# A two-product MLP beside a windowed attention: blocks of 512 tokens in place of 256, and the second product token tile by token tile

## The chip, the cores and the metric

The kernel runs on one core of one Trainium2 chip. That core has TensorE (matrix products, with its own queue of weight loads, called PEld in the profile), VectorE (DVE), ScalarE (ACT), GpSimd (POOL), and SyncE (SP), which here only issues DMAs. Each engine works through its own instructions in the order in which the program gives them; engines wait for each other through semaphores. The metric is the device time of one execution in microseconds (us). Lower is better.

## The reference, cut to what matters

There are 2048 tokens of width 576. They are normalized, and two branches are added to the input:

```python
x = A_x                                       # 1 x 2048 x 576
xn = _layernorm(x, axis=-1)
# branch A: 32 heads of 18; each token looks at itself and at 7 tokens, 2 apart, before it
qkv = xn @ wqkv;  logits = q . k over the window * 18**-0.5;  o = softmax(logits) . v;  A = o @ wo
# branch B
h = jnp.maximum(xn @ w1, 0)                   # 576 -> 4608
B = h @ w2                                    # 4608 -> 576
return x + A + B
```

All is float32. The kernel gets precision near float32 from TensorE's fast float32 mode by splitting every operand into a high part and a low part, which is what the rounding of the high part left over. A product is then three products: high x high, low x high and high x low.

## The kernel before

**Tiling.** Tokens are taken in two phases of 1024 (even and odd tokens, so that the dilated window becomes a plain one). A phase has 8 token tiles of 128 tokens. For branch B a phase has 4 blocks of 256 tokens (two token tiles each). The 4608 columns of w1 are 36 F tiles of 128, and three F tiles make a chunk, so there are 12 chunks. The innermost loops are: phase, chunk, block, F tile of the chunk. One turn of these four loops is a *slot*; there are 288.

**One slot.** `h_mm` (line 438) makes the first product for one F tile and one block: 14 matmuls (list `TERMS`: 576 rows are four and a half tiles of 128, high and low) with a 128x128 tile of w1 as weights, streaming the block's 256 columns of x^T (tile xT) into a PSUM tile `ph`. Then ACT writes the high part of the relu (`hhi`, line 447) and DVE the low part (`hlo`, line 448). `o_mm` (line 453) makes the second product for the same F tile: for both token tiles of the block, six matmuls of 288 columns with 128x128 pieces of hhi or hlo as weights and w2 streaming, into a PSUM tile `po` per token tile. The two `po` collect over the three F tiles of the chunk; at the third, DVE adds them to the token tile of x in SBUF (line 471), which thus becomes the output. `h_mm` runs two slots ahead of `o_mm` (`LAG`).

**The order.** All engines' instructions are issued in an order written out by hand. A slot issues: the weight splits that are due (`run_splits`), `h_mm`, the steps that `at` has put on this slot, `o_mm`, the steps that `late` has put there, and background work (`run_bg`). A plan gives each step its slot:
- *weights*: `w1_task`, `w2_task`, `wq_tasks`, `wo_tasks` queue a load from HBM into a staging tile `st` (SP) and, at their slot, a split (`two`, line 146: ACT copies the high part; line 143: DVE subtracts for the low part). `stage_more` keeps `AHEAD` = 3 loads ahead in four staging tiles; they are used in order of their step numbers.
- *x*: `load_x` (SP), `stats` (mean and variance on DVE, then two small POOL steps), `norm` (on DVE, line 259, or with `act` on ACT, lines 256 and 257; a last small ACT copy, line 261, follows), `make_xt` (five TensorE transposes, then ACT high parts, lines 276 and 278, and DVE low parts, lines 277 and 279).
- *branch A*: four units of 8 heads, 27 slots apart: `qkv_tile` (14 matmuls of 432 columns for each token tile into a `pm`, three ACT copies), then `attention`, whose DVE steps wait in a list `bg`. `run_bg` issues them as long as the program's own estimate of DVE's time is at most a margin ahead of its estimate of TensorE's. `wo_a` and `wo_b` make the last product of branch A.

PSUM has 8 banks: two `po` tiles of two banks, two `ph`, and two `pm` for everything else.

**The start.** Before the first slot the tiles of x and the first weights are loaded, tiles 0 and 1 are normalized and transposed, and the first w1 tiles are split. The list `HEAD` then places the statistics, norms and transposes of tiles 2 to 7 on slots -2 to 5, and `HEADW` the first six weight splits on slots -5 to 1. The first block needs only tiles 0 and 1, the second only 2 and 3. 24 transposes of the identity (`WARM`) run on TensorE at the very start.

Of the kernel before, what the change touches and what calls it, by code (L numbers as in the profile page):

```python
# [20 lines left out]
NTB = 4  # L21
TBN = 256
# [4 lines left out]
LAG = 2  # L27
# [3 lines left out]
HEADW = (-5, -2, -1, 0, 0, 1)  # L31

HEAD = (
    (-2, 0, 'stats', 3),
    (-2, 1, 'xt', 2, True),
    (-1, 0, 'stats', 4),
    (-1, 1, 'norm', 3, True),
    (0, 0, 'xt', 3, False),
    (0, 0, 'norm', 4, True),
    (0, 0, 'stats', 6),  # L40
    (0, 1, 'stats', 5),
    (1, 1, 'norm', 5, False),
    (1, 1, 'xt', 4, False),
    (2, 1, 'xt', 5, False),
    (2, 1, 'norm', 6, True),
    (2, 1, 'stats', 7),
    (4, 0, 'norm', 7, True),
    (4, 1, 'xt', 6, False),
    (5, 1, 'xt', 7, False),
)  # L50
HALO = ((0, 112), (112, 127))
# [4 lines left out]
def tile_body(ctx: ExitStack, tc: tile.TileContext, x, wqkv, wo, w1, w2, out):  # L56
# [11 lines left out]
    SPC = NTB * C  # L68
# [13 lines left out]
    stp = pool("stp", 4)  # L82
    hp = pool("hp", LAG + 2)
    prp = pool("prp", 2)
    lgp = pool("lgp", 2)
# [3 lines left out]
    ps_h = pool("ps_h", 2, space=PSUM)  # L89
    ps_m = pool("ps_m", 2, space=PSUM)  # L90
# [20 lines left out]
    def mm(o, l, r, start, stop, n):  # L111
        nc.tensor.matmul(o, l, r, start=start, stop=stop)  # L112
        t["pe"] += n / 2400.0 + 0.002
# [7 lines left out]
    AHEAD = 3  # L121
# [142 lines left out]
    def transpose_split(src, last, hi, mix, lo, free=False):  # L264

        if free:
            pa, pb = (ps_o.tile([P, 2, 512], F32, name="po")[:, 0, :] for _ in range(2))
            pa, pb = pa.rearrange("p (k c) -> p k c", k=KT), pb[:, 0:P]
        else:
            pa = ps_m.tile([P, KT, P], F32, name="pm")  # L270
            pb = ps_m.tile([P, P], F32, name="pm")
# [11 lines left out]
    def make_xt(ph, i, free=False):  # L283
        tb, h = divmod(i, 2)
# [12 lines left out]
    def qkv_tile(ph, u, i):  # L297
# [9 lines left out]
        tb, h = divmod(i, 2)  # L307
        xt = XT[ph, tb]
        pq = ps_m.tile([P, 3, UD], F32, name="pm")
# [97 lines left out]
    def wo_a(ph, i):  # L407
        assert (ph, i) in ready, (ph, i, len(bg))
        o = QO[ph][:, i, :]
        od = tmp.tile([P, 2, DR], F32, name="od")  # L410
# [5 lines left out]
    def wo_b(ph, i):  # L416
        d, w = OT.pop((ph, i)), WO[ph]
        po = [ps_m.tile([P, D2], F32, name="pm") for _ in range(2)]
# [15 lines left out]

    slots = [(ph, c, tb, f) for ph in range(NPH) for c in range(NCH) for tb in range(NTB) for f in range(C)]
    H, PO = {}, {}

    def h_mm(n):
        ph, c, tb, f = slots[n]
        w, xt = W1[ph, c, f], XT[ph, tb]  # L440
        pt = ps_h.tile([P, TBN], F32, name="ph")
# [7 lines left out]
        t["dve"] = max(t["dve"], t["pe"] + 0.6)  # L449
        dve(TBN)  # L450
        H[n] = (hi, lo)
# [76 lines left out]
    for i in range(AHEAD + 2, NI):  # L528
        load_x(0, i)
# [56 lines left out]
```

## Time and profile before

| what | value |
|---|---|
| time, median of 3 runs | 1194.94 us (1194.33 to 1195.93) |
| the profiled execution's own time | 1194.74 us |
| its span in the trace | 1193.0 us |
| TensorE busy | 1183.8 us (99%) |
| weight loads (PEld) busy | 1172.8 us (98%) |
| DVE busy | 812.5 us (68%) |
| ACT busy | 310.5 us (26%) |
| POOL busy | 40.1 us (3%) |
| DMA moved | 75.67 MB, mean 63 GB/s |

How to read the profile: each row of the groups is one kind of instruction, as line, engine, operation, output<-inputs with the partitions x elements, a count, then total busy time, mean ns of one, and idle time of the engine just before them with what ended it. In the timeline a row is a start, a length, and a group of like instructions; the length runs to the modelled end of the last one, and matmuls overlap, so the pace of matmuls is read from one start to the next. The chain of waits follows the work back from the last instruction, at each step to what released it.

### The profile page before, as it was taken

How to read it: one execution, taken by the hardware profiler on the slowest of the kernel's cores; microseconds unless marked ns; L12 is line 12 of the kernel's file. 1: busy time of each engine (PE TensorE's matmuls, PEld its weight loads, DVE VectorE, ACT ScalarE, POOL GpSimd, SP SyncE). 2: the span in 40 equal slices, each digit the busy share in tenths (PEclk: the TensorE clock that was granted, in tenths of full speed). 3: DMA queues.
4: the chain of work that ended last, by engine and by line, in shares of the span. 5: the costliest groups of instructions: out<-in, count | busy, mean ns of one | idle time of the engine just before them, and what ended most of it. 6: DMA issues, size and time to landing. Idle time of an engine off the chain costs nothing.

```text
span 1193.0 us, 21739 instructions
## 1 busy us (share of the span) xinstructions
PE 1183.8 (99%) x9016; PEld 1172.8 (98%) x9016; DVE 812.5 (68%) x1269; ACT 310.5 (26%) x790; POOL 40.1 (3%) x63
## 2 busy tenths in 40 slices
PE   8999999999999999999999999999999999999998
PEld 7999999999999999999999999999999999999998
DVE  7516875888687578875573278858767875886732
ACT  5422222131222222322233123122221322222210
POOL 2000000010000000000120000000100000000000
PEclk9999999999999999999999999999999999999999
DMA  5312122130321311402242113031302312212002
GB/s 172 84 32 82 42 76 55 38 107 1 98 58 44 86 33 43 114 11 73 91 130 74 46 54 90 22 85 29 86 21 79 83 38 79 63 42 73 21 1 80
DMA packets 84883, 75.67 MB, mean 63 GB/s; under 512 B 6592, under 2 KB 68288, under 8 KB 84784
## 3 DMA queue, kind: packets, MB, share of 16 engines
q1 hardware_dynamic: 82256, 66.08, 19.7%
q10 hardware_dynamic: 2528, 8.20, 2.4%
q8 instruction: 71, 1.16, 0.4%
q14 instruction: 28, 0.23, 0.1%
HBM read 61.34 MB, written 4.72 MB: 55 GB/s over the span
## 4 chain that ended last, share of the span: by engine, by line
PE 98%; DVE 1%; SPq 0%; ACT 0%; DMA 0%; issue 0%; DVEq 0%; ACTq 0%
PE ph L112 39%; PE po L112 38%; PE pm L112 20%; PE pm L273 1%; PE pm L274 0%; DMA st<-in_w 0%; SPq L235 0%; DVE pr L380 0%; DVE pr L373 0%; SPq L157 0%; SPq L162 0%; SPq L161 0%; PE po L273 0%; ACT xn L257 0%; ACT xn L256 0%
## 5 line engine op out<-in xcount | busy, mean ns | idle before, releaser
L112 PE MATMUL ph<-xT,w1t 128*128 128x256 f32 x4032 | 514.2, 279 | 1.3 <-ACT xT L276 0.6
L112 PEld LDWEIGHTS ph<-xT,w1t 128*128 128x128 f32 x4032 | 491.6, 188 | 2.0 <-ACT xT L276 0.8
L112 PE MATMUL po<-w2t,hhi 128*128 128x288 f32 x2304 | 400.5, 296 | 0.4 <-DVE w2t L143 0.3
L112 PEld LDWEIGHTS po<-w2t,hhi 128*128 128x128 f32 x2304 | 337.0, 188 | 2.0 <-DVE w2t L143 0.5
L447 ACT ACTIVATE hhi<-ph 128x256 fp32r<-128x256 f32 x288 | 110.2, 382 | 531.8 <-PE ph L112 512.5
L112 PE MATMUL po<-w2t,hlo 128*128 128x288 f32 x1152 | 244.7, 293 | 0.0
L448 DVE SCALAR_TENSOR_TENSOR hlo<-ph,hhi 128x256 fp32r<-128x256 f32 x288 | 121.7, 423 | 169.1 <-ACT hhi L447 167.8
L471 DVE TENSOR_TENSOR x<-po,x 128x576 f32<-128x576 f32 x192 | 143.9, 757 | 69.8 <-PE po L112 66.3
L112 PE MATMUL pm<-wq,xT 128*128 128x432 f32 x896 | 185.5, 358 | 0.0
L112 PEld LDWEIGHTS po<-w2t,hlo 128*128 128x128 f32 x1152 | 183.7, 188 | 0.0
L112 PEld LDWEIGHTS pm<-wq,xT 128*128 128x128 f32 x896 | 163.8, 188 | 5.6
L343 DVE TENSOR_TENSOR pr<-qo,k 128x1152 f32<-128x1152 f32 x64 | 85.9, 1349 | 0.0
L373 DVE TENSOR_TENSOR pr<-lg,v 128x1152 f32<-128x1152 f32 x64 | 85.0, 1352 | 0.3
L346 DVE TENSOR_REDUCE lg<-pr 128x64 f32<-128x1152 f32 x64 | 85.0, 1343 | 0.0
L143 DVE TENSOR_TENSOR w2t<-st,w2t 128x576 fp32r<-128x576 f32 x72 | 54.3, 755 | 45.0 <-ACT w2t L146 44.7
L380 DVE TENSOR_TENSOR pr<-pr 128x288 f32<-128x288 f32 (+1 forms) x128 | 70.5, 602 | 0.1
L143 DVE TENSOR_TENSOR w1t<-st,w1t 128x640 fp32r<-128x640 f32 x72 | 59.0, 820 | 15.0 <-ACT w1t L146 14.8
L146 ACT ACTIVATE w2t<-st 128x576 fp32r<-128x576 f32 x72 | 49.1, 684 | 45.0 <-PE po L112 31.0
L146 ACT ACTIVATE w1t<-st 128x640 fp32r<-128x640 f32 x72 | 53.0, 737 | 13.2 <-DMA st<-in_w 13.2
L312 ACT ACTIVATE k<-pm 128x144 f32<-128x144 f32 x64 | 18.7, 292 | 142.8 <-PE pm L112 142.6
L112 PE MATMUL pm<-wq,oT 128*128 128x288 f32 x352 | 51.7, 299 | 0.0
L112 PEld LDWEIGHTS pm<-wq,oT 128*128 128x128 f32 x352 | 47.9, 188 | 1.7
(63 smaller groups left out, 398.0 us busy)
## 6 DMA issues: line engine op xcount, KB each, us to landing
st<-in_w SPq DMA_DIRECT2D x72, 288.0 KB, 3.0
st<-in_w SPq DMA_DIRECT2D x72, 256.0 KB, 3.0
st<-in_wqkv SPq DMA_DIRECT2D x32, 216.0 KB, 3.0
st<-in_w SPq DMA_DIRECT2D x144, 32.0 KB, 2.7
out<-x SPq DMA_DIRECT2D x16, 288.0 KB, 2.1
x<-in_x SPq DMA_DIRECT2D x15, 288.0 KB, 3.9
k<-k ACTq DMA_DIRECT2D x8, 441.0 KB, 3.9
v<-v ACTq DMA_DIRECT2D x8, 441.0 KB, 4.6
```

Source lines behind the costliest of these rows:

```text
L112: nc.tensor.matmul(o, l, r, start=start, stop=stop)
L143: nc.vector.tensor_tensor(lo, src, f32(hi), op=ALU.subtract)
L146: nc.scalar.activation(hi, src, AF.Copy)
L273: nc.tensor.transpose(pa[:, k, :], src[:, k * P : (k + 1) * P], ident)
L312: nc.scalar.activation(k[:, W - 1 + i, :], pq[:, 1, :], AF.Copy)
L343: nc.vector.tensor_tensor(pr[i], q, window(k, i), op=ALU.mult)
L346: nc.vector.tensor_reduce(lg[:, i], pr.pop(i).rearrange(heads, d=Dh), axis=AX.X, op=ALU.add)
L373: nc.vector.tensor_tensor(pr[i].rearrange(heads, d=Dh), e, window(v, i).rearrange(heads, d=Dh), op=ALU.mult)
L380: nc.vector.tensor_tensor(o, z[:, 0:n], z[:, n : 2 * n], op=ALU.add)
L447: nc.scalar.activation(hi, pt, AF.Relu)
L448: nc.vector.scalar_tensor_tensor(lo, pt, 0.0, f32(hi), op0=ALU.max, op1=ALU.subtract)
L471: nc.vector.tensor_tensor(acc, PO[k][:, :, 0:D2], acc, op=ALU.add)
```

## The change

The names changed are few, but the order of nearly all work changes with them.
- A block is 512 tokens: four token tiles (`TBT`), two blocks in a phase (`NTB`). `h_mm` streams 512 columns into one whole PSUM bank, and the relu's two parts are 128x512 each.
- A block's turn (`SPB`) is six slots. In the first three, `h_mm` runs for the F tiles 1 and 2 of this block and F tile 0 of the next. In the last three the second product runs, a third of it in each (`o_mm`, now drawing from the generator `o_pieces`): token tile by token tile, and for each token tile all three F tiles, so that one `po` is filled by 18 matmuls in a row and then added to x. A phase still has 144 slots, and the slots of the weights' and of branch A's steps are nearly those of before.
- PSUM: `ph` and `pm` share one pool of four banks (`ps_x`). Staging tiles are 3 in place of 4, loads ahead 2 in place of 3, and the softmax tile `lg` has one buffer.
- `run_bg` is called inside `h_mm` after every four matmuls and inside `o_mm` after every six, with one margin of 2.0 us; the estimates of TensorE's and DVE's time have new constants.
- The start is written out anew. F tile 0 and F tile 1 of the first block are made in halves of 256 columns (`A`, `B`), with the transposes of tiles 2 and 3 between them; the second product of the first block stands in slots 3 to 5, and the transposes of tiles 5, 6 and 7 stand at the head of its three slots. The third w2 tile's split has the step number 3.
- The x tiles of the second phase are prepared on slots that fit the new blocks.

The diff, cut to its core:

```diff
-NTB = 4
-TBN = 256
+NTB = 2
+TBT = 4
+TBN = TBT * P
-LAG = 2
-HEADW = (-5, -2, -1, 0, 0, 1)
+HEADW = (-9, -8, -7, -6, -5, 3)
 HEAD = (
...
+    (3, 0, "xt", 5),
+    (3, 0, "stats", 6),
+    (3, 1, "norm", 6),
+    (3, 1, "stats", 7),
+    (4, 0, "xt", 6),
+    (4, 1, "norm", 7),
+    (5, 0, "xt", 7),
 )
+MARGIN = 2.0
-    SPC = NTB * C
+    SPB = 2 * C
+    SPC = NTB * SPB
-    stp = pool("stp", 4)
-    hp = pool("hp", LAG + 2)
+    stp = pool("stp", 3)
+    hp = pool("hp", C + 1)
-    lgp = pool("lgp", 2)
+    lgp = pool("lgp", 1)
-    ps_h = pool("ps_h", 2, space=PSUM)
-    ps_m = pool("ps_m", 2, space=PSUM)
+    ps_x = pool("ps_x", 4, space=PSUM)
-        t["pe"] += n / 2400.0 + 0.002
+        t["pe"] += n / 2250.0 + 0.0025
-    AHEAD = 3
+    AHEAD = 2
...
+    def h_mm(n, f, cols=slice(0, TBN)):
+        ph, c, tb = blocks[n]
         w, xt = W1[ph, c, f], XT[ph, tb]
+        if cols.start == 0:
+            PH[n, f] = ps_x.tile([P, TBN], F32, name="px")
+        pt = PH[n, f]
         for j, (a, b) in enumerate(TERMS):
             wb = w[:, b // 5, (b % 5) * P : (b % 5 + 1) * P]
-            mm(pt, wb, xt[:, a, :], j == 0, j == len(TERMS) - 1, TBN)
+            mm(pt[:, cols], wb, xt[:, a, cols], j == 0, j == len(TERMS) - 1, cols.stop - cols.start)
+            if j % 4 == 3:
+                run_bg(MARGIN)
+        if cols.stop < TBN:
+            return
...
+    def o_pieces(n):
+        ph, c, tb = blocks[n]
+        for k in range(TBT):
+            po = ps_o.tile([P, 2, 512], F32, name="po")
             cs = slice(k * P, (k + 1) * P)
+            for f in range(C):
+                hi, lo = H[n, f]
+                w = W2[ph, c, f]
+                for j, (l, b) in enumerate(((hi, 0), (hi, 1), (lo, 0))):
+                    for h in range(2):
+                        mm(
+                            po[:, h, 0:D2], l[:, cs], w[:, b, h * D2 : (h + 1) * D2],
+                            f == 0 and j == 0, f == C - 1 and j == 2, D2,
+                        )
+                        if f == C - 1 and j == 2 and h == 1:
+                            i = TBT * tb + k
+                            acc = X[ph, i].rearrange("p (h c) -> p h c", h=2)
+                            nc.vector.tensor_tensor(acc, po[:, :, 0:D2], acc, op=ALU.add)
...
+                        yield
...
+    def o_mm(n, s):
+        if s == 0:
+            PO[n] = o_pieces(n)
+        for i in range(6 * TBT):
+            next(PO[n])
+            if i % 6 == 5:
+                run_bg(MARGIN)
...
+                plan.append((HEADW[f] if first else s - 8 + (0, 4, 5)[f], w1_task, ((ph, c, f), c * C + f)))
+                plan.append((HEADW[C + f] if first else s + (-2, 0, 1)[f], w2_task, ((ph, c, f), c * C + f)))
...
+    run_splits(-9)
     norm(0, 0)
     norm(0, 1)
     stats(0, 2)
...
     norm(0, 2, True)
+    h_mm(0, 0, A)
+    stats(0, 3)
+    run_splits(-8)
+    make_xt(0, 2, True)
+    norm(0, 3, True)
+    h_mm(0, 1, A)
+    run_splits(-7)
+    make_xt(0, 3, True)
+    h_mm(0, 0, B)
+    stats(0, 4)
+    h_mm(0, 1, B)
+    norm(0, 4, True)
+    h_mm(0, 2)
+    run_splits(-6)
+    stats(0, 5)
+    make_xt(0, 4)
+    run_splits(-5)
+    norm(0, 5)
...
+    for n in range(C, len(blocks) * SPB):
         run_splits(n)
+        q, s = divmod(n, SPB)
+        if s < C - 1:
+            if n == SPB:
+                h_mm(1, 0)
+            h_mm(q, s + 1)
+        elif s == C - 1 and q + 1 < len(blocks):
+            h_mm(q + 1, 0)
         for f, a in todo.pop(n, []):
             f(*a)
+        if s >= C:
+            o_mm(q, s - C)
         for f, a in todo_late.pop(n, []):
             f(*a)
+        run_bg(MARGIN)
```

More of the change, by code (lines that the diff above doesn't have):

```diff
@@ L417, in wo_b @@
         d, w = OT.pop((ph, i)), WO[ph]
-        po = [ps_m.tile([P, D2], F32, name="pm") for _ in range(2)]
+        po = [ps_x.tile([P, 512], F32, name="px")[:, 0:D2] for _ in range(2)]
         for j, (a, b) in enumerate(TERMS):
@@ L477, in tile_body @@
+    def o_mm(n, s):
[5 more added lines that the diff above has]
+                run_bg(MARGIN)
+        if s == C - 1:
+            assert next(PO.pop(n), None) is None
     todo = {}
```

99 lines of the change are left out of this document (27 added, 72 removed).

## The prediction

> **What bounds the kernel now.** I read the page first: busy shares, then the chain that ended last.
>
> ```profile
> span 1193.0 us, 21739 instructions
> ...
> PE 1183.8 (99%) x9016; PEld 1172.8 (98%) x9016; DVE 812.5 (68%) x1269; ACT 310.5 (26%) x790; POOL 40.1 (3%) x63
> ...
> PE 98%; DVE 1%; SPq 0%; ACT 0%; DMA 0%; issue 0%; DVEq 0%; ACTq 0%
> PE ph L112 39%; PE po L112 38%; PE pm L112 20%; PE pm L273 1%; PE pm L274 0%; DMA st<-in_w 0%; SPq L235 0%; DVE pr L380 0%; DVE pr L373 0%; SPq L157 0%; SPq L162 0%; SPq L161 0%; PE po L273 0%; ACT xn L257 0%; ACT xn L256 0%
> ```
>
> TensorE is the chain: 98% of it. The first product (tile ph) is about 39% of the span, 465 us, or 115 ns for each of its 4032 matmuls. A matmul's own duration is no pace, since they overlap; the pace stands in the starts. The timeline of TensorE:
>
> ```profile
> 300.65 1.77 PE L112 MATMUL ph<-xT,w1t 128*128 128x256 f32 x14
> 302.25 2.90 PE L112 MATMUL pm<-wq,xT 128*128 128x432 f32 x14
> 304.99 0.70 PE L112 MATMUL po<-w2t,hhi 128*128 128x288 f32 x4
> ...
> 306.57 1.76 PE L112 MATMUL ph<-xT,w1t 128*128 128x256 f32 x14
> ```
>
> 256 columns: (302.25 - 300.65) / 14 = 114.3 ns. 432 columns: (304.99 - 302.25) / 14 = 195.7 ns. 288 columns: (306.57 - 304.99) / 12 = 131.7 ns. Per column that is 0.446, 0.453 and 0.457 ns: the wide ones are no cheaper. The view by stage shows where TensorE rests:
>
> ```profile
> 11.20:14.30 3.10, 3.10 (x15) 3.02 (x16) 1.86 (x4) 1.42 (x3) 0.00 (x0) 0.50 1.00 346
> 14.60:20.00 5.40, 4.83 (x37) 4.04 (x35) 5.11 (x14) 4.89 (x11) 1.73 (x4) 1.00 0.45 156
> ...
> 620.00:1180.00 560.00, 559.95 (x4267) 555.38 (x4266) 378.06 (x570) 137.41 (x354) 12.91 (x14) 1.00 0.20 56
> ```
>
> Columns: stage, its length, busy time of PE, PEld, DVE, ACT, POOL, then granted clock and DMA. In mid-kernel TensorE is busy 559.95 of 560 us: no wait is left there to remove. Waits stand in the first 20 us, where DVE (5.11 of 5.40) and ACT (4.89) are full too. So the change can act through the price of a 512-column matmul, and through the order of the first block.
>
> **The change part by part.** *Price of the first product.* 4032 matmuls of 256 columns become 2016 of 512 (28 of them, in the first block, stay 56 halves of 256); the columns are the same. No row has 512. Two more rows bound it, the same timeline in two windows while the clock was 0.50 (row above):
>
> ```profile
> 11.99 1.64 PE L112 MATMUL ph<-xT,w1t 128*128 128x256 f32 x6
> ...
> 12.20 1.42 PE L112 MATMUL ph<-xT,w1t 128*128 128x256 f32 x5
> ```
>
> Six from 11.99 and five from 12.20 end together at 13.62: one took 0.21 us at half clock, so 105 ns at full clock, 0.41 ns per column. What the rows at full clock have above that: 9 ns at 256 (114.3 - 105), 14 at 288 (131.7 - 118), 19 at 432 (195.7 - 177). For 512 the columns are 210 ns; the ends are 219 (the surplus of 256) and 231.3 (the line through 288 and 432, 0.444 ns per column). I take 228.5, the surplus of the nearest row, 432. 2016 x 228.5 = 460.7 against 4032 x 114.3 = 460.8: nothing, with ends of -19 and +6. That half the weight loads go is costed at nothing: PEld runs beside PE, and the columns set the pace at 288 and 432.
>
> The Trainium skill ("TensorE: Matmul & The Clock Gate", Back-to-back issue gap) has columns / 2.4 GHz + 2.5 ns; it gives 215.8 ns at 512, and the first product would lose 26 us. The same rule gives 122.5 at 288 and 182.5 at 432, where this trace has 131.7 and 195.7, so the trace does not agree.
>
> *Second product.* The same 3456 matmuls of 288 columns in runs of 72 instead of 12: nothing. Accumulations stay 192.
>
> *Evictions.* The durations by form:
>
> ```profile
> L471 DVE TENSOR_TENSOR x<-po,x 128x576 f32<-128x576 f32 x192 | 143.9, 757 | 69.8 <-PE po L112 66.3
> L448 DVE SCALAR_TENSOR_TENSOR hlo<-ph,hhi 128x256 fp32r<-128x256 f32 x288 | 121.7, 423 | 169.1 <-ACT hhi L447 167.8
> L447 ACT ACTIVATE hhi<-ph 128x256 fp32r<-128x256 f32 x288 | 110.2, 382 | 531.8 <-PE ph L112 512.5 <-DMA k<-k 18.1 <-DVE qo L380 0.9
> ...
> L143 DVE TENSOR_TENSOR w1t<-st,w1t 128x640 fp32r<-128x640 f32 x72 | 59.0, 820 | 15.0 <-ACT w1t L146 14.8
> L143 DVE TENSOR_TENSOR w2t<-st,w2t 128x576 fp32r<-128x576 f32 x72 | 54.3, 755 | 45.0 <-ACT w2t L146 44.7
> L146 ACT ACTIVATE w1t<-st 128x640 fp32r<-128x640 f32 x72 | 53.0, 737 | 13.2 <-DMA st<-in_w 13.2
> ...
> L146 ACT ACTIVATE w2t<-st 128x576 fp32r<-128x576 f32 x72 | 49.1, 684 | 45.0 <-PE po L112 31.0 <-DMA st<-in_w 8.1 <-issue 5.9
> ...
> L143 DVE TENSOR_TENSOR wq<-st,wq 128x432 fp32r<-128x432 f32 x40 | 23.9, 598 | 7.9 <-ACT wq L146 7.8
> ...
> L277 DVE TENSOR_TENSOR xT<-pm,xT 128x512 fp32r<-128x512 f32 x14 | 9.6, 688 | 3.9 <-ACT xT L276 3.9
> ...
> L276 ACT ACTIVATE xT<-pm 128x512 fp32r<-128x512 f32 x14 | 8.3, 594 | 2.7 <-PE pm L273 2.7
> ...
> L259 DVE TENSOR_SCALAR xn<-x,nm,rstd 128x576 f32<-128x576 f32 x11 | 6.9, 626 | 0.8 <-POOL rstd L248 0.7
> ...
> L279 DVE TENSOR_TENSOR xT<-pm,xT 64x128 fp32r<-64x128 f32 x14 | 4.1, 295 | 0.4
> ```
>
> With the 128x512 rows as prices (ACT 594, DVE 688 ns) 288 x (382 + 423) ns becomes 144 x (594 + 688): 47 us less on ACT and DVE, both off the path. The low half is due at the earliest 3.2 us later (the next block's first F tile lies between) and takes 1.3 us: hidden. A po tile is needed again after the 18 matmuls of the next, 2.37 us, and its accumulation takes 0.76: hidden, unless DVE is behind (a rival). In the shared PSUM pool of four, a buffer comes round after at least three other tiles: hidden.
>
> *Fewer buffers.* Two x^T tiles, three staging tiles, one softmax tile. In mid-kernel a weight is split two to four slots (6 us or more) before its use and its load is issued a split earlier: hidden. At the phase change x^T, statistics and loads are three to eight slots ahead: hidden, with 0 to +3 us as ends.
>
> *The first block.* Here nothing covers. TensorE needed tiles 2 and 3 only for its fourth group; now the second half of the first group needs them, and all other steps stand behind each other on ACT and DVE, which work in order. The chain and timeline of before have the other durations:
>
> ```profile
> 14.66 1.62 PE ph L112 x14
> ...
> 16.58 0.78 ACT xn L256
> ...
> 17.44 0.79 ACT xn L257
> ...
> 18.25 0.26 ACT xn L261
> ...
> 19.93 1.59 PE po L112 x10
> ```
>
> ```profile
> 14.42 0.81 DVE L243 BATCH_NORM_STATS2 bst<-x 128x6 f32<-128x288 f32 x2
> 14.51 0.60 ACT L276 ACTIVATE xT<-po 128x512 fp32r<-128x512 f32 x1 [0.47 <-PE po L273]
> 15.01 0.27 ACT L278 ACTIVATE xT<-po 128x128 fp32r<-128x128 f32 x1
> ...
> 15.51 0.15 DVE L245 TENSOR_SCALAR mv<-mv 128x1 f32<-128x1 f32 x1
> ...
> 15.74 0.57 POOL L248 TENSOR_TENSOR rstd<-mv,mhalf 128x1 f32<-128x1 f32 x1
> ...
> 19.11 1.43 DVE L143 TENSOR_TENSOR w2t<-st,w2t 128x576 fp32r<-128x576 f32 x2
> ```
>
> Statistics take 1.24 us on DVE (14.42 to 15.66), 1.9 with POOL (to 16.31). Up to the transposes of tile 2 the order is as before, so I go on from 14.5 us by these rows:
> (a) ACT: copies of tile 2 to 15.3, norm of tile 3 (0.78 + 0.79 + 0.26) to 17.1. TensorE ends the first half of group 1 at 16.2 and waits 0.7. ACT: split of w1's third tile to 17.9, copy of tile 3 to 18.5: TensorE waits 1.0 more. DVE: that split (0.82) to 18.7, low parts of tile 3 (0.69, 0.30) to 19.7: it waits 0.75. Sum 2.5.
> (b) Rest of group 0, group 1's second half and group 2 end near 25.6, tile 4's transposes near 26.6 (0.3 waiting). Tile 4's statistics come behind group 0's low half, so its norm on ACT ends near 26.0 and group 2's relu near 26.6. Then DVE goes through low half 0.69, w2 split 0.76, statistics 1.24, tile 4's low parts 0.98, w2 split 0.76, norm of tile 5 0.63: 5.1 us, to 31.7. The transposes of tile 5 stand in TensorE's queue ahead of the second product, so all of that waits 5.1.
> (c) The third w2 tile has the step number 3, behind two wqkv splits, and its load needs the staging tile that the second w2 split frees at 31.1:
>
> ```profile
> st<-in_w SPq DMA_DIRECT2D x72, 288.0 KB, 3.0
> ```
>
> It lands at 34.1, is copied by 34.8 and split by 35.5. TensorE, after 0.55 us of transposes and 12 matmuls (1.6), is there at 33.9 and waits 0.9 + 0.4 = 1.3. Behind that load SP holds only later weights.
> (d) Tile 6's norm stands behind tile 5's low parts 0.98, statistics 1.24 and the first accumulation 0.76: it ends at 39.1, TensorE waits from 36.8: 2.3. Tile 7's stands behind statistics 1.24, two splits (0.60 + 0.82), low parts 0.98, accumulation 0.76: 0.63 after that is 44.1, TensorE is there at 42.8: 1.3.
> Sum 2.5 + 0.3 + 5.1 + 1.3 + 2.3 + 1.3 = 12.8 us. The waits of before in this stretch go: from 14.66 to 19.93 it did two groups (3.2), five transposes (0.55) and two matmuls (0.26), so 1.2. Net 11.6; instructions that follow each other on DVE overlap a little (two splits 1.43 against 1.51), over some fifteen 0.6. I take +11. Ends: +6 (half of the 10.3 of (b) to (d) hides otherwise) and +14 (the clock falls to 0.50 after the 5 us of rest, as it did at 11 us, and 3.1 us go at half speed).
>
> *Sum.* The profiled run took 1194.74 us, 0.2 below the median of 1194.94. First product 0, second 0, evictions 0, mid-kernel 0, first block +11: 1205.7 us.
>
> **The rivals.**
> 1. *Columns become cheap (faster).* The 256-column matmul may be held by its weight load (PEld 98% busy), and 512 columns free it. For: 0.41 ns per column at half clock. Against: 288 and 432 have the longer columns and still 14 and 19 ns surplus. At 219 ns: 1205.7 - 19 = 1186.7. It decides from 2016 x r = 460.8 - 13.4, r = 221.9 ns, on. Chance 0.17. (By the 215.8 ns of the Trainium skill, the page named above, it would be 1180.)
> 2. *The first block costs little (same).* If tile 5's norm were not held behind DVE, the 5.1 us and most of (c) and (d) would shrink; with (a) alone it is 2.5 - 1.2 = 1.3: 1196. Cases in which a price of 222 to 224 ns makes up for the first block count here too. Against: DVE was busy 5.11 of 5.40 us already. Chance 0.11.
> 3. *Accumulations become the bound (slower yet).* The background is put up to 2.0 us ahead on DVE. If it is there in full at a tile's end, 2.0 + 0.76 exceeds the 2.37 us, and the third and fourth tile of a block wait 0.4 each: 96 x 0.4 = 38 us at worst, a third of it likely: 1218. Against: the cost model adds background only after six matmuls (0.79 us). Chance 0.10.
>
> **How the numbers follow.** Forecast (wide columns at 225 to 232 ns, first block +8 to +14): chance 0.62, 1205.7, own range 1198 to 1213. Slower by over 0.2% (2.4 us, about what a measurement of this kernel can tell) is forecast and rival 3, 0.72; same is rival 2, 0.11; faster is rival 1, 0.17. Range 1186 to 1214: it takes in most of rival 1, and leaves out its cheaper end (0.08) and the worse of rival 3 (0.08).
>
> **What would show it.** Starts of the 512-column matmuls 225 to 232 ns apart (rival 1: under 222). Idle TensorE between 14 and 45 us of 10 to 14 us, most of it ahead of tile 5's transposes, put down to DVE xn; a clock under 1 after it. From 60 us on, TensorE full as before; waits of PE on DVE x at the third tile would be rival 3. Wrong it would be most simply by the price of 512 columns: each 5 ns is 10 us.

## The result, and the profile after

| | time, median | ratio to the kernel before, 95% interval |
|---|---|---|
| before, runs beside it | 1195.28 us (1194.33 to 1195.93) | |
| after | 1237.39 us (1236.84 to 1238.74) | 1.0355 [1.0337, 1.0373] |

The change costs 42 us. The forecast was 1205.7 us with 1186 to 1214: the sign was right, the size was not, by 31.7 us.

The busy times on the page of after:

```profile
PE 1199.4 (97%) x7028; PEld 1092.2 (88%) x7028; DVE 793.3 (64%) x1127; ACT 285.0 (23%) x642; POOL 39.6 (3%) x63
```

ACT and DVE together have 44.7 us less to do than before, near the 47 of the forecast. But TensorE now has rests. What it waited for (the view of waits of after: us in total, times, longest):

```profile
PE po L104 <- DVE x L471: 12.3, 11, 3.2
PE px L265 <- DVE xn L251: 7.8, 4, 5.0
PE px L104 <- ACT oT L268: 5.8, 10, 0.6
```

The second row stands in the first block. The first and third stand behind it, from 265 us on, where the forecast had put nothing. Where: the view by stretches (length, then busy time of PE, PEld, DVE, ACT, POOL, then granted clock), first of before, then of after.

```profile
1.00:50.00 49.00, 44.92 (x326) 43.03 (x327) 34.26 (x78) 27.33 (x62) 9.94 (x20) 0.97 0.48 142
255.00:275.00 20.00, 20.00 (x142) 19.71 (x141) 15.34 (x22) 4.66 (x14) 3.17 (x3) 1.00 0.23 63
500.00:640.00 140.00, 139.92 (x1106) 138.69 (x1105) 89.35 (x180) 38.39 (x101) 9.82 (x18) 1.00 0.25 74
1.00:1193.00 1192.00, 1183.77 (x9016) 1172.81 (x9016) 812.54 (x1269) 310.20 (x790) 39.71 (x58) 1.00 0.22 63
```

```profile
1.00:50.00 49.00, 36.04 (x211) 32.60 (x212) 32.47 (x72) 21.74 (x47) 9.38 (x20) 0.90 0.46 130
255.00:275.00 20.00, 16.82 (x98) 15.51 (x97) 14.83 (x21) 6.68 (x12) 2.85 (x3) 0.91 0.36 94
500.00:640.00 140.00, 134.73 (x860) 123.03 (x859) 85.38 (x162) 35.38 (x80) 10.49 (x18) 1.00 0.25 75
860.00:885.00 25.00, 22.00 (x120) 19.69 (x119) 19.94 (x28) 8.10 (x14) 2.85 (x3) 0.93 0.37 100
1.00:1235.90 1234.90, 1199.41 (x7028) 1092.24 (x7028) 793.28 (x1127) 284.69 (x642) 39.20 (x58) 0.99 0.22 61
```

TensorE's rest grew from 1192 - 1183.8 = 8.2 us to 1234.9 - 1199.4 = 35.5, by 27.3; its busy time grew by 15.6. Together that is the 42.9 us by which the span grew. The rest: 8.9 in the first 50 us (44.92 - 36.04), 3.2 + 3.0 near 265 and 870 us, 1.2 near 331 us and as much again near 936, 5.2 from 500 to 640 us (139.92 - 134.73), and some 5 in smaller pieces. The busy time: the lower clock is 0.07 x 49 + 0.09 x 20 + 0.07 x 25 = 7.0 us; the price of the first product comes to 5 (below); 3.6 us are not assigned.

The stall at 265 us is the one to learn from. The timeline of after there, and further pieces of the same view that are used below:

```profile
32.95 1.09 PE L265 MATMUL px<-ident,xn 128*128 128x128 f32 x4 [4.99 <-DVE xn L251]
...
261.54 0.82 DVE L135 TENSOR_TENSOR w1t<-st,w1t 128x640 fp32r<-128x640 f32 x1
...
262.39 0.37 SPq L149 DMA_DIRECT2D st<-in_w  x1
...
262.81 1.14 DVE L354 TENSOR_REDUCE r<-lg 128x64 f32<-128x512 f32 x1
...
263.98 0.56 DVE L357 RECIPROCAL r<-r 128x64 f32<-128x64 f32 x1
...
264.45 0.63 DVE L448 SCALAR_TENSOR_TENSOR hlo<-px,hhi 128x512 fp32r<-128x512 f32 x1
...
264.99 0.60 DVE L135 TENSOR_TENSOR wq<-st,wq 128x432 fp32r<-128x432 f32 x1
...
265.93 0.74 ACT L138 ACTIVATE w1t<-st 128x640 fp32r<-128x640 f32 x1 [3.03 <-DMA st<-in_w]
266.70 0.82 DVE L135 TENSOR_TENSOR w1t<-st,w1t 128x640 fp32r<-128x640 f32 x1 [1.11 <-ACT w1t L138]
...
267.44 0.75 DVE L471 TENSOR_TENSOR x<-po,x 128x576 f32<-128x576 f32 x1
...
268.24 0.53 PE L104 MATMUL po<-w2t,hhi 128*128 128x288 f32 x2 [3.18 <-DVE x L471]
...
327.73 1.73 ACTq L310 DMA_DIRECT2D v<-v  x2
329.56 0.74 ACT L138 ACTIVATE w1t<-st 128x640 fp32r<-128x640 f32 x1 [3.00 <-issue]
...
331.88 0.80 PE L104 MATMUL po<-w2t,hhi 128*128 128x288 f32 x4 [1.23 <-DVE x L471]
...
528.81 0.27 PE L266 MATMUL px<-ident,od 128*128 128x128 f32 x1
529.66 0.53 PE L104 MATMUL px<-wq,oT 128*128 128x288 f32 x2 [0.58 <-ACT oT L268]
...
657.04 6.70 PE L104 MATMUL px<-xT,w1t 128*128 128x512 f32 x28
663.58 0.74 PE L104 MATMUL px<-wq,xT 128*128 128x432 f32 x3
```

Read it from 261.54 us on. DVE's split of a w1 tile ends at 262.36 and frees a staging tile; only then SP issues the next w1 load, at 262.39; ACT waits 3.03 us for it; DVE's part of that split ends at 267.5. The accumulation (L471) of a `po` that TensorE had filled by about 262.7 stands behind this split in DVE's order, so it ran only at 267.44; and TensorE, which needs that `po` back for the third token tile of the block, rested 3.18 us, from 265.06 to 268.24. The page's waits name DVE, but part of what came late was a DMA, held by a staging tile.

Only part of it. From 262.8 us on DVE does two steps of the softmax (L354, L357: 1.7 us), the low half of an F tile and a wqkv split; then it waits 1.11 us for the late w1 split and does that. So of TensorE's 3.18 us of rest DVE waits in 1.11 and works in 2.07. At 870 us it is 0.94 of 3.00; in the nine shorter rests DVE hardly waits (0.2 us together). What makes the accumulations late is thus mostly the work that DVE's order puts ahead of them, and in two places a late load on top.

At 331 us a `po` is held by another head of a queue: ACT issues its DMAs (L310) for 3 us, the split behind them starts late, and so does the accumulation behind the split.

The rests lower the clock as well. Two short stretches of after:

```profile
33.00:36.90 3.90, 3.90 (x17) 3.90 (x18) 2.19 (x4) 2.33 (x6) 0.00 (x0) 0.50 0.61 157
269.00:272.40 3.40, 3.40 (x17) 3.40 (x16) 2.38 (x5) 0.84 (x2) 0.00 (x0) 0.50 0.66 134
```

After the rest of 4.99 us, 3.9 us go at clock 0.50, and after that of 3.18, 3.4 us: 1.9 and 1.7 us of work are lost. The Trainium skill ("TensorE: Matmul & The Clock Gate", What's actually happening) has the half clock follow at least one idle window of about 3.4 us; the length of the second slow stretch agrees, and here a rest of 3.18 us was enough.

### The profile page after: what moved, and what is told of

Same layout as the page of the kernel before. It is cut to its first block, busy times and chain, and to the rows that moved or that the text cites. A ratio compares the mean times of both kernels' runs of the same rounds, so it can differ in the third digit from the quotient of the medians.

```text
span 1235.9 us, 17259 instructions
## 1 busy us (share of the span) xinstructions
PE 1199.4 (97%) x7028; PEld 1092.2 (88%) x7028; DVE 793.3 (64%) x1127; ACT 285.0 (23%) x642; POOL 39.6 (3%) x63
## 5 line engine op out<-in xcount | busy, mean ns | idle before, releaser
L104 PE MATMUL px<-xT,w1t 128*128 128x512 f32 (+1 forms) x2044 | 485.7, 394 | 2.6 <-ACT xT L268 1.4
L104 PEld LDWEIGHTS px<-xT,w1t 128*128 128x128 f32 x2044 | 379.0, 189 | 87.9 <-ACT xT L268 1.8
L104 PE MATMUL po<-w2t,hhi 128*128 128x288 f32 x2304 | 403.2, 297 | 12.4 <-DVE x L471 12.3
L104 PEld LDWEIGHTS po<-w2t,hhi 128*128 128x128 f32 x2304 | 342.1, 190 | 19.7 <-DVE x L471 16.4
L471 DVE TENSOR_TENSOR x<-po,x 128x576 f32<-128x576 f32 x192 | 144.6, 753 | 146.4 <-PE po L104 145.6
L448 DVE SCALAR_TENSOR_TENSOR hlo<-px,hhi 128x512 fp32r<-128x512 f32 x144 | 99.3, 689 | 157.3 <-ACT hhi L447 156.2
L447 ACT ACTIVATE hhi<-px 128x512 fp32r<-128x512 f32 x144 | 86.0, 597 | 475.7 <-PE px L104 462.0
L104 PE MATMUL px<-wq,xT 128*128 128x432 f32 x896 | 184.7, 358 | 0.0
L104 PEld LDWEIGHTS px<-wq,xT 128*128 128x128 f32 x896 | 166.9, 188 | 9.2
L304 ACT ACTIVATE k<-px 128x144 f32<-128x144 f32 x64 | 18.6, 291 | 193.4 <-PE px L104 193.4
L104 PE MATMUL px<-wq,oT 128*128 128x288 f32 x352 | 50.1, 297 | 5.8 <-ACT oT L268 5.8
L104 PEld LDWEIGHTS px<-wq,oT 128*128 128x128 f32 x352 | 47.5, 188 | 8.7 <-ACT oT L268 8.1
```

Source lines behind the costliest of these rows:

```text
L304: nc.scalar.activation(k[:, W - 1 + i, :], pq[:, 1, :], AF.Copy)
L447: nc.scalar.activation(hi, pt, AF.Relu)
L448: nc.vector.scalar_tensor_tensor(lo, pt, 0.0, f32(hi), op0=ALU.max, op1=ALU.subtract)
L471: nc.vector.tensor_tensor(acc, po[:, :, 0:D2], acc, op=ALU.add)
```

## The experiments

Each run starts from the changed kernel unless it is said otherwise. Theory: the 31.7 us that the forecast lacks come from accumulations held behind weight splits in DVE's order, with staging as the cause, and from pauses in branch A's last product. Rivals: they come from the 512-column matmul, or from the first block.

**spread, stage2, stage4 and w2p3: is it the splits that wait for their loads?** spread moves only the splits of wqkv and wo: two slots apart instead of one, and beginning six slots earlier.

```diff
-            f([step + k for k in range(5)], *a)
+            wide = f is wo_tasks or a[0] != (0, 0)
+            f([step - 6 + 2 * k if wide else step + k for k in range(5)], *a)
```

> The changed kernel with one edit: the five splits of each wqkv or wo group go two slots apart and begin six slots earlier, so that they no longer fall on the same slots as the w1 and w2 splits (only the first group keeps its slots). Theory A (TensorE's waits on DVE x come from accumulations that stand on DVE behind a weight split whose load came late, for want of a free staging tile): the waits of 3.2 us at 265 and 870 us go, PE's wait on DVE x falls from 12.3 us to under 5, the clock stays at full speed there, and the time falls by 7 to 12 us, to 1225 to 1230. Theory B (DVE is over-full with background work put 2.0 us ahead, wherever the splits are): the waits stay at 10 to 14 us and the time within 3 us of 1237.

Measured: 1224.07 us, 13.3 less, where 7 to 12 were expected; ratio to before 1.0247 [1.0232, 1.0262]. Its waits, and the stretch at 265 us:

```profile
PE po L104 <- DVE x L471: 5.6, 7, 1.4
...
255.00:275.00 20.00, 20.00 (x119) 17.96 (x118) 19.37 (x26) 6.42 (x11) 2.86 (x3) 1.00 0.33 89
```

The rest at 265 us is gone, and the half clock with it (at 870 us the same), though DVE's busy time in that stretch rose from 14.83 to 19.37 us. So it is not the amount of DVE's work there that counts, but what stands ahead of an accumulation: theory B falls as the whole cause. The waits fell by 6.7 us, and the clock near 265 and 870 us gives 3.6. Some 1.2 us more are not the edit's: in the first block, whose order it leaves alone, the eighth accumulation starts at 84.33 us here and at 85.49 in after, since the half clock fell differently there. The edit takes splits out of the accumulations' way and gives their loads more time at once, so it can't tell which of the two did it.

stage2 takes one more staging tile away:

```diff
-    stp = pool("stp", 3)
+    stp = pool("stp", 2)
-    AHEAD = 2
+    AHEAD = 1
```

> The changed kernel with two staging tiles in place of three (and one load ahead in place of two): the suspected shortage made worse, the order of all else the same. Theory (splits wait for late loads, accumulations stand behind them on DVE, TensorE finds no free po): PE's wait on DVE x grows from 12.3 us to over 25 us, at more places than the eleven of the changed kernel and first where wqkv and w splits meet, and the time rises by 12 us or more, over 1249. Rival (the two waits of 3.2 us were a matter of slots alone, not of staging): the time rises by less than 5 us.

stage4 gives the fourth staging tile back. For room it takes one w2 tile, and a control, w2p3, does that alone:

```diff
-    w2p = pool("w2p", C + 1)
+    w2p = pool("w2p", C)
-    stp = pool("stp", 3)
+    stp = pool("stp", 4)
-    AHEAD = 2
+    AHEAD = 3
...
-                plan.append((HEADW[C + f] if first else s + (-2, 0, 1)[f], w2_task, ((ph, c, f), c * C + f)))
+                plan.append((HEADW[C + f] if first else s + (0, 0, 1)[f], w2_task, ((ph, c, f), c * C + f)))
```

> Control for the run stage4: the changed kernel with three w2 buffers in place of four and the first two w2 splits of a chunk on the chunk's first slot (steps 0, 0, 1 in place of -2, 0, 1), which makes room in SBUF. No theory expects a gain: 1230 to 1245, PE's wait on DVE x 10 to 16 us.

> The control (three w2 buffers, w2 steps 0, 0, 1) with the fourth staging tile and the three loads ahead of the kernel before; all slots are the control's. Theory (late loads for want of a staging tile): the waits of 3 us or more near 265 and 870 us go, PE's wait on DVE x falls by 5 us or more against the control, the time by 6 to 10 us. Rival (two splits on one slot are enough, wherever their loads are): within 3 us of the control.

Measured: stage2 1253.68 us (1.0492 [1.0473, 1.0511]); w2p3 1238.45; stage4 1230.34 (1.0296 [1.0279, 1.0313]), 8.1 below its control. The row of waits of stage2, of w2p3 and of stage4, and the same stretch of stage4:

```profile
PE po L104 <- DVE x L471: 21.2, 12, 4.2
```

```profile
PE po L104 <- DVE x L471: 13.3, 10, 3.5
```

```profile
PE po L104 <- DVE x L471: 10.2, 9, 2.0
...
255.00:275.00 20.00, 18.00 (x109) 16.18 (x108) 17.43 (x24) 6.90 (x13) 2.85 (x3) 1.00 0.33 85
```

With two, three and four staging tiles the wait is 21.2, 13.3 and 10.2 us: it follows the staging, in order (after, from which stage2 starts, has 12.3). The sizes were missed: stage2's wait was expected over 25 us, and the fourth tile takes 3.1 us of waiting, not 5. What is left in stage4 shows why. DVE's rows there:

```profile
264.97 0.82 DVE L135 TENSOR_TENSOR w1t<-st,w1t 128x640 fp32r<-128x640 f32 x1
265.71 0.75 DVE L471 TENSOR_TENSOR x<-po,x 128x576 f32<-128x576 f32 x1
```

The load is in time now: this split starts without a wait, at the end of the wqkv split before it. The accumulation behind it is late all the same, by the work ahead of it, and TensorE rests 2.0 us where it rested 3.2 in the control. But at 2.0 us no half clock follows: the clock is 1.00 in that stretch and near 870 us, where the control has 0.83 and 0.93, and that is the other 5 of the 8.1 us. The splits' spacing does more than the fourth tile: spread took 6.7 us of waits away with three.

**wo: the pauses of branch A's last product.** `wo_b` and `done` move behind the second product in their slot.

```diff
-            at(s + i + 1, wo_b, ph, i)
-            at(s + i + 1, done, ph, i)
+            late(s + i + 1, wo_b, ph, i)
+            late(s + i + 1, done, ph, i)
```

> The changed kernel with one edit: the last product of branch A (wo_b) comes behind the slot's second product instead of ahead of it, so that it no longer follows its own transposes at once. Theory: the ten pauses of 0.85 us between the transposes and that product (PE waits on ACT oT, 5.8 us in the table) go, and with them 7 to 9 us: 1228 to 1231. Rival: the pause only moves, to a wait of the product for DVE's low parts or of the next transposes for PSUM, and the time stays within 2 us.

Measured: 1228.97 us, 8.4 less (1.0288 [1.0271, 1.0305]), some 1.2 of it in the first block as in spread. The wait on oT has left the list of waits. The stretch across the phase change:

```profile
500.00:640.00 140.00, 137.32 (x878) 126.03 (x877) 86.43 (x165) 37.76 (x86) 10.50 (x18) 1.00 0.26 80
```

In after, ten times the matmuls of `wo_b` stand in TensorE's order directly behind the transposes of `wo_a` that make their oT, since three of a block's six slots have no `h_mm` between the two. TensorE does one transpose in the 0.85 us from 528.81 to 529.66 us, and waits for ACT's copy. In before a run of the first product covers that copy:

```profile
520.02 0.27 PE L274 MATMUL pm<-ident,od 128*128 128x128 f32 x1
520.05 1.85 PE L112 MATMUL ph<-xT,w1t 128*128 128x256 f32 x14
521.74 3.23 PE L112 MATMUL pm<-wq,oT 128*128 128x288 f32 x22
```

With the second product between, as the edit has it, the wait is gone.

**head and head2: the first block.** head puts tile 5's statistics and norm ahead of the third group, the third w2 split earlier, and the transposes of tiles 5 to 7 behind the second product.

```diff
-HEADW = (-9, -8, -7, -6, -5, 3)
+HEADW = (-9, -8, -7, -6, -5, -4)
-    (3, 0, "xt", 5),
+    (3, 1, "xt", 5),
-    (4, 0, "xt", 6),
+    (4, 1, "xt", 6),
-    (5, 0, "xt", 7),
+    (5, 1, "xt", 7),
...
+    stats(0, 5)
+    norm(0, 5)
     h_mm(0, 2)
...
-    stats(0, 5)
+    run_splits(-5)
+    run_splits(-4)
     make_xt(0, 4)
-    run_splits(-5)
-    norm(0, 5)
```

> The changed kernel with the first block's order changed: statistics and norm of tile 5 ahead of the third group on DVE, the third w2 split two splits earlier (step -4), the transposes of tiles 5, 6 and 7 behind the second product of their slot. Theory: the wait of 5.0 us ahead of tile 5's transposes, those of 1.7 and 0.9 for tiles 6 and 7, and the half clock from 30 to 37 us go; what is lost by 50 us falls from 25.4 to 14 to 18 us, and the time by 7 to 11 us, to 1226 to 1230. Rival: the splits of w2 take the place of the norm, another wait of 4 us or more stands at the second product, and the time falls by less than 4 us.

head2 makes the first chunk in half blocks of 256 columns (`h_first`, `o_first`), with the lists `HEAD` and `HEADW` of the kernel before.

```diff
+    for n in range(-2, SPC):
+        run_splits(n)
+        if n + 2 < SPC:
+            h_first(n + 2)
+        elif n + 1 == SPC:
+            h_mm(2, 0)
+        for f, a in todo.pop(n, []):
+            f(*a)
+        if n >= 0:
+            o_first(n)
+        for f, a in todo_late.pop(n, []):
+            f(*a)
+        run_bg(MARGIN)
```

> The changed kernel with one part undone: the first chunk of the first phase (the first two blocks) goes in half blocks of 256 tokens in the order of the kernel before, with its lists HEAD and HEADW; from slot 12 on all is as in the changed kernel. Theory: the first block's cost is its order alone; what is lost by 50 us falls from 25.4 us to 12.5 to 14.5 (before: 12.8), the two windows of half clock between 20 and 37 us go, and the time falls by 11 to 13 us, to 1224 to 1227. Rival: three staging tiles in place of four hold the first splits as well; then 17 us or more stay lost and the time stays over 1229.

Measured: head 1235.99 us, 1.4 less (1.0344 [1.0329, 1.0359]); head2 1227.84, 9.6 less (1.0273 [1.0259, 1.0287]). Waits of head, and the first stretch of head2:

```profile
PE po L104 <- DVE x L471: 16.5, 13, 3.4
...
PE po L104 <- ACT w2t L138: 1.5, 1, 1.5
```

```profile
1.00:50.00 49.00, 44.60 (x322) 42.12 (x322) 33.94 (x78) 27.45 (x62) 9.40 (x20) 1.00 0.47 136
```

head took the wait for tile 5's norm away and got others: TensorE waits 4.2 us more for accumulations than in after, 3.1 of them in the first block, and 1.5 us for a w2 split. The first block still ends 3 us sooner (its eighth accumulation starts at 82.51 us, in after at 85.49), but near 265 us the half clock lasts longer (0.83 in that stretch, 0.91 in after), and little of it is left at the end. head2 has TensorE busy for 44.60 us where before has 44.92, and its eighth accumulation starts at 73.16 us, in before at 72.57. So the first block of 512 costs about 10 of the 42 us by the times (11 to 13 were expected) and 12.3 by this mark, and the rival that the missing 31.7 us lay there falls: the forecast had 11 for it.

**halves: the price of 512 columns.** Each run of 14 matmuls of 512 columns becomes two runs of 14 of 256; all else stays.

```diff
+        for lo in range(cols.start, cols.stop, TBN // 2):
+            cs = slice(lo, lo + TBN // 2)
+            for j, (a, b) in enumerate(TERMS):
+                wb = w[:, b // 5, (b % 5) * P : (b % 5 + 1) * P]
+                mm(pt[:, cs], wb, xt[:, a, cs], j == 0, j == len(TERMS) - 1, TBN // 2)
```

> The changed kernel with one edit: each first product of 512 columns is made as two runs of 14 matmuls of 256 columns into the two halves of the same PSUM tile; the order of everything else is kept. If the price of the wide matmul is 233.4 ns against two of 113.5 to 115, 1988 x 3.4 to 6.4 ns = 7 to 13 us go: 1224 to 1230. If the wide matmul costs nothing more than two narrow ones in this order, the time stays within 3 us of 1237. If the weight loads had been what the wide form saved, it rises.

Measured: 1235.44 us, 2 less (1.034 [1.0325, 1.0355]), where the price by itself would have given 7 to 13. From start to start the first product takes 467.6 us in all, 8.8 less than in after, so narrow columns are the cheaper ones; but TensorE came to the second product sooner and waited there, 2.2 us more than in after, and near 870 us the clock fell to 0.86 from 0.93, 1.7 us more. Some 3 us of what was lost again are not traced.

```profile
PE po L104 <- DVE x L473: 14.5, 11, 4.7
```

**price and price2: the matmul by itself.** price issues only groups of 14 matmuls with the kernel's weight pattern, in widths from 128 to 512 columns, while the other engines rest; the tiles of x^T and of the weights start on multiples of 128 bytes. Each of the two was executed once.

```diff
+    for n in (128, 256, 288, 320, 384, 432, 448, 480, 512, 256, 512):
+        for _ in range(12):
+            pt = ps.tile([P, 512], F32, name="pt")
+            for j, (c, d) in enumerate(terms):
+                nc.tensor.matmul(pt[:, 0:n], wr[:, d, :], xr[:, c, 0:n], start=j == 0, stop=j == len(terms) - 1)
```

> Not the computation: TensorE alone. After a few loads, for 128, 256, 288, 320, 384, 432, 448, 480, 512, 256 and 512 columns each, 12 groups of 14 matmuls with the terms' order of the first product, every operand in the fast float32 form, while ACT, DVE and the DMA queues rest; then x is copied out with the last PSUM tile added. If the surplus over 0.41 ns per column comes from other engines' traffic, 512 columns take 214 to 220 ns here and 288 and 432 take 121 to 125 and 181 to 186. If it is TensorE's own, they take 229 to 236, 130 to 134 and 193 to 198, and 256 stays at 113 to 115.

price2 does the same for 256 and 512 columns while the weights (a) and the streamed operand (b) start at other offsets, in elements of 4 bytes:

```diff
+    cases = [(0, 0, 512)] * 3 + [(a, b, n) for a in (0, 16) for b in (0, 8, 16, 32, 48) for n in (256, 512)]
...
+                w0, x0 = a + d * P, b + c * 512
+                nc.tensor.matmul(
+                    pt[:, 0:n], wr[:, w0 : w0 + P], xr[:, x0 : x0 + n], start=j == 0, stop=j == len(terms) - 1
+                )
```

> Not the computation: TensorE alone as in the run price, with 256 and 512 columns, while the start addresses move: the weights by 0 or 64 bytes, the streamed operand by 0, 32, 64, 128 or 192 bytes against a 128-byte boundary (in the kernels before and after, the x^T tiles start 64 bytes off such a boundary and the w1 tiles on it; in the run price both start on it). Theory C (the price of a matmul hangs on where its operands lie): with the streamed operand 64 or 192 bytes off, 512 columns take 230 to 236 ns and 256 take 113 to 116, as in the kernels; on the boundary 226.7 and 120.0, as in price. Theory D (the 6.7 ns above 226.7 come from the other engines' traffic): 226.7 and 120.0 at every address.

Stretches of price (288 and 256 columns), and of price2 (512 columns, with x 0, 128 and 192 bytes beyond the weights' start):

```profile
80.00:98.00 18.00, 18.00 (x139) 18.00 (x138) 0.00 (x0) 0.00 (x0) 0.00 (x0) 1.00 0.00 1
296.00:314.00 18.00, 18.00 (x153) 18.00 (x152) 0.00 (x0) 0.00 (x0) 0.00 (x0) 1.00 0.00 1
```

```profile
112.00:136.00 24.00, 24.00 (x108) 19.86 (x107) 0.00 (x0) 0.00 (x0) 0.00 (x0) 1.00 0.00 1
228.00:252.00 24.00, 24.00 (x105) 19.45 (x104) 0.00 (x0) 0.00 (x0) 0.00 (x0) 1.00 0.00 0
268.00:292.00 24.00, 24.00 (x105) 19.23 (x104) 0.00 (x0) 0.00 (x0) 0.00 (x0) 1.00 0.00 1
```

The length of a stretch by its count, less the two or so that only reach into it, is near the pace. In price, from the starts themselves, 288 columns took 131.7 ns and 432 took 195.8, as in the kernels. So the surplus over the columns is TensorE's own, not the traffic of other engines. But 512 took 226.7 and 256 took 120.0, where this theory expected 229 to 236 and 113 to 115; price2 was made for that. (The 128 columns stand in the first 60 us, in which TensorE ran more slowly, with 213.3 ns for 128 and 256 columns alike; they are not used.) price2, in ns:

| start of weights, of x (bytes) | x beyond the weights, modulo 256 | 256 columns | 512 columns |
|---|---|---|---|
| 0, 0 (price too) | 0 | 120.0 | 226.7 |
| 64, 64 | 0 | 120.0 | 226.7 |
| 0, 32 | 32 | 116.7 | 233.3 |
| 0, 64 | 64 | 113.4 | 228.9 |
| 64, 128 | 64 | 117.8 | 228.9 |
| 0, 128 | 128 | 120.0 | 232.4 |
| 64, 192 | 128 | 118.7 | 233.3 |
| 0, 192 | 192 | 117.8 | 233.3 |
| 64, 0 | 192 | 113.4 | 233.3 |
| 64, 32 | 224 | 118.4 | 233.3 |

The price hangs on where the two operands start. Sorted by the distance between the two starts, modulo 256 bytes, the 512 columns fall in order: 226.7 ns at 0, 228.9 at 64, 232.4 to 233.3 at all others. For 256 columns the distance alone doesn't decide (113.4 and 117.8 at 192).

In the kernels the pools xtp, qop, kp and vp lie between the first x^T tile and the first w1 tile: 36864 + 18432 + 8640 + 17280 = 81216 bytes of a partition, 64 beyond a multiple of 256. So x stands at 192, where 512 columns take 233.3 ns alone; the 233.4 of the kernel leaves next to nothing for other engines' traffic.

**best and best_wide: all mended together.** best_wide is spread, wo and head2 in one, and the copies at L310 issued by POOL's queue instead of ACT's; best has the halves as well.

```diff
-                    nc.scalar.dma_start(z[a + 1 : b + 1, 0 : W - 1, :], z[a:b, NI : NI + W - 1, :])
+                    nc.gpsimd.dma_start(z[a + 1 : b + 1, 0 : W - 1, :], z[a:b, NI : NI + W - 1, :])
```

> The same as the run best, but with 512-column first products: the price of the wide matmul in an order with few waits. If one wide matmul costs 233.4 ns and two narrow ones 227 to 229, it takes 1964 x 4.4 to 6.4 ns = 9 to 13 us longer than best, 1199 to 1210. If the wide matmul's cost in the changed kernel came from that order, within 3 us of best.

> The edits together: wqkv and wo splits two slots apart and six slots earlier, wo_b behind the second product, 256-column first products, the first chunk in half blocks as before, and the halo copies of k and v issued from POOL's queue in place of ACT's. If the costs found singly add up: 1237.4 - 13.3 - 8.4 - 2 to 9 (price of the columns) - 11 to 13 - 2.8 (the two waits of 1.4 us at 325 and 923 us behind ACT's DMA issues) = 1190 to 1199; PE's wait on DVE x under 5 us. If they hide each other, over 1203.

Measured: best_wide 1202.11 us (1.006 [1.0048, 1.0073]), best 1199.36 (1.0036 [1.0023, 1.005]). Waits of best_wide:

```profile
PE po L113 <- DVE x L516: 3.1, 5, 1.4
```

The mends together give 35.3 of the 42 us back. What stays in best_wide is mostly price: from 60 us on its 512-column matmuls start 233.5 ns apart on the mean, where two of before's 256-column ones take 2 x 115.44 = 230.9; times 1932 that is 5.0 of the 6.8 us. The copies' new queue was not run alone; in spread rests of 1.2 us still stand near 325 and 923 us, in best_wide there are none near there.

best is 2.8 us faster than best_wide, not the 9 to 13 that the wide price was expected to cost. The price is there: from 60 us on the first product takes 8.5 us less in best (114.5 ns a matmul). But its 288-column matmuls start 134.7 ns apart on the mean, in before 133.2, which is 5.6 us. Some 4 us of these are a few rests, such as the 3.6 us that TensorE waits on DVE x (L518); without the steps that hold a rest the means are 133.5 and 133.1.

**after_al, before_al, best_wide_al: does the start matter in the kernel itself?** One line is moved in each, so that the x^T tiles start on a multiple of 128 bytes instead of 64 beyond one (the tiles of qo and k move with them):

```diff
+    kp = pool("kp", 1)
     xtp = pool("xtp", NTB)
...
-    kp = pool("kp", 1)
```

> The changed kernel with one line moved: the pool kp is made before the pool xtp, so that the x^T tiles start on a multiple of 128 bytes and no longer at 64 beyond one; the weights stay where they are. Theory C (the price of a matmul hangs on where its operands start): 1988 matmuls of 512 columns go from 233.4 ns to the 226.7 ns that both operands on such a boundary gave by themselves, 13 us less, 1224 us. Rival (the starts don't matter in the kernel, since other work sets the pace there): 233 ns, within 3 us of 1237.

> The kernel before with the same line moved. Theory C: its 256-column matmuls go from 113.3 ns to 120.0 ns, 4032 times 6.7 ns or 27 us more, 1222 us. Rival: 113 ns, within 3 us of 1195.

> best_wide with the same line moved. Theory C: 226.7 ns instead of 233.4 ns for its matmuls of 512 columns, 13 us less than its 1202 us: 1189 us, below the kernel before. Rival: 1199 to 1205 us, 233 ns as it was.

Measured: before_al 1206.17 us (1.0096 [1.0082, 1.0109], 11.5 us over before), after_al 1239.76 (1.0378 [1.0364, 1.0392], 2.4 over after), best_wide_al 1204.96 (1.0087 [1.0073, 1.01], 2.9 over best_wide). The timeline of TensorE in before_al, then in after_al:

```profile
684.27 1.82 PE L112 MATMUL ph<-xT,w1t 128*128 128x256 f32 x14
685.92 0.69 PE L112 MATMUL po<-w2t,hhi 128*128 128x288 f32 x4
```

```profile
657.03 6.66 PE L104 MATMUL px<-xT,w1t 128*128 128x512 f32 x28
663.53 2.92 PE L104 MATMUL px<-wq,xT 128*128 128x432 f32 x14
```

before_al: (685.92 - 684.27) / 14 = 117.9 ns, against 114.3; from 60 us on the mean went from 115.4 to 118.8, which is 13.5 us for 4032. So the start does set the narrow matmul's price in the kernel, with the expected sign and half the size. after_al: 6.50 / 28 = 232.1 against (663.58 - 657.04) / 28 = 233.6; the mean went from 233.4 to 233.1. The wide matmul did not fall to 226.7 ns, and what little it gained was lost in the other products, which moved by up to 0.9 ns.

The table tells why. With kp moved, 81216 - 8640 = 72576 bytes lie between x^T and w1, 128 beyond a multiple of 256. At a distance of 128 the table has 118.7 to 120.0 ns for 256 columns and 232.4 to 233.3 for 512, and the kernels have 118.8 and 233.1. The expectations, 120.0 and 226.7, took the row of distance 0, since they counted modulo 128. So theory C fits both widths. This was read from the table after the runs; a kernel with x^T at distance 0, which by the table would bring 226.7 ns, was not run. No version here beats the kernel before.

## Why the prediction was wrong

**Price of the first product.** Taken at 228.5 ns, measured 233.4, above the upper end of 231.3. Against the mean of before, 115.4 from 60 us on (the forecast took 114.3 from one row), the step is +5 us instead of 0. A fixed surplus over the columns was too simple: the surplus depends on the starts of the operands too. Rival 1, cheap columns, did not come. Nor did the issue-gap rule of the Trainium skill ("TensorE: Matmul & The Clock Gate", Back-to-back issue gap): its 215.8 ns at 512 columns were not reached even by TensorE alone (226.7).

**Second product.** Costed at nothing for itself, and its matmuls kept their pace within 2 ns; its waits belong to the next step.

**Evictions, the step that failed.** The text has: "A po tile is needed again after the 18 matmuls of the next, 2.37 us, and its accumulation takes 0.76: hidden, unless DVE is behind (a rival)." The durations were right, but the accumulation does not start when its `po` is full: it starts when DVE has done what stands ahead of it, 4.7 us later at 265 us. The sum put this at nothing. It cost 12.3 us of rest and 3.6 us of clock. With `po` finished one at a time every 2.4 us, TensorE has less slack for a late one than when two were finished at the end of a chunk's third F tile; this last reason is argued, not shown.

Rival 3 had the sign of it, waits on DVE x at a block's third tile, and part of the cause, background work ahead of the accumulation (1.7 us of it at 265 us). The splits and the late load were not in it. Its likely price, a third of 38 us, is near the 12.3 by luck: it was to come from 96 rests of 0.4 us and came from eleven, two of them of 3 us.

**Fewer buffers, a part of the same.** That "its load is issued a split earlier: hidden" failed where w1 and wqkv splits fall on neighbouring slots. There, with three staging tiles, the load could be issued only when a tile came free at 262.36 us, and ACT could start on it 3.5 us later. The fourth tile was worth 3.1 us of waits and 5 of clock (stage4 against w2p3).

**The first block.** Predicted +11, with +6 and +14 as ends; measured 8.9 us of rest and 3.4 of clock, and head2 gives 9.6 back. This part held, and its single steps came close: 5.1 us ahead of tile 5's transposes were 4.99. From 14 to 45 us TensorE was idle for 9.9 us, where 10 to 14 were named as the sign. The upper end added the whole 3.1 us of a stretch at half clock, of which only half is lost; but two such stretches came, at 19.8 to 23.3 us and at 33.0 to 36.9.

**Not in the sum at all.** Branch A's last product, whose transposes and matmuls now follow each other on TensorE (5.8 us of waits, 8.4 by the run), and the DMA issues on ACT (two rests of 1.2 us). "In mid-kernel TensorE is busy 559.95 of 560 us: no wait is left there to remove", and from it "So the change can act through the price of a 512-column matmul, and through the order of the first block": this is where they were lost. That there is no wait to remove says nothing about waits that a new order puts in.

Evictions (15.9 us), branch A (about 7, without the 1.2 in the first block) and the price (5) make some 28 of the 31.7 us; the rest is not traced.

## What to carry to other kernels

Where a change reorders the issue of an engine that works in order, walk each queue at its densest place, and ask of every eviction what stands directly ahead of it: background steps and splits delay it by their own time, and a split that waits for a load delays it by that wait too. An engine at 64% busy can hold one at 97%, and here a rest of three microseconds cost TensorE at least half as much again in clock. Before a matmul's price is carried from one width to another, measure it, with the operands where the kernel has them.

## What the runs showed of the hardware

- The same fast float32 matmul, with nothing else running, took 113.4 to 120.0 ns for 256 columns and 226.7 to 233.3 for 512, by the start addresses of its operands alone. For 512 columns it was 226.7 where both start at the same place modulo 256 bytes, 228.9 with x 64 bytes further, and 232.4 to 233.3 at the other distances tried. In the kernel before, moving the x^T tiles from 192 to 128 bytes beyond the weights, modulo 256, cost 11.5 us of 1195.
- A rest of 3.18 us was followed by 3.4 us at half clock (after, near 265 us); at rests of up to 2.0 us (stage4, near 265 us) the clock stayed at 1.00.
